# First mixture of experts: a 128-column arm for slots of 128 rows or fewer, and w1 split by column halves

## The chip, the cores and the metric

The kernel runs on one core of a Trainium2 chip. Its engines are TensorE (PE; its weight loads are listed as PEld), VectorE (DVE), ScalarE (ACT), GpSimd (POOL) and SyncE (SP, which only issues transfers). Each has an instruction queue of its own; semaphores order them. The metric is the device time of one execution in microseconds (us).

## The reference

Three layers follow each other, all in float32: a linear attention over 4 x 8 heads of 576 x 64, and two mixtures of experts over N = 2304 rows of 512. The change touches the first mixture, in which some rows are skipped and each of the others goes to one expert:

```python
do_compute = (x @ w_skip) > 0
xc = x[do_compute]
e_idx = argmax(xc @ w_gate)          # one of 8 experts for each row
gate_w = softmax(xc @ w_gate)[e_idx]
h = relu(xc[mask] @ w1[e])           # w1[e]: 512 x 1024
y[mask] = gate_w * (h @ w2[e])       # w2[e]: 1024 x 512
out[do_compute] = xc + y             # the other rows stay x
```

The second mixture is dense, takes most of the time, and starts from the rows that the first one has written to DRAM.

## The kernel before

`moe1` (line 583) works through slots: up to 256 rows (`SLOT`) of one expert. Attention leaves, in DRAM, the rows of x with their gates (`x2d`) and for each expert a list of row numbers (`idx`). Slots 0 and 1 are filled early, from the rows known by then. The others are planned on the chip by `slots` (line 536): first all full slots, those with more than 128 rows (`nfull` of them), then those with 128 or fewer; `nslots` counts both. These two numbers are registers that branches read. `chain` (line 759) nests the slots from 2 up to 17, each under `tc.If(nslots > s - 2)`; the first that fails leaves the chain, and the second mixture begins.

A product in near float32 accuracy is made of three matmuls on a rounded type (float32r): high by high, high by low, low by high, where high is the rounded operand and low the rest. So each operand is split: ACT writes the high half, DVE the low one. In one slot (`slot_body`, line 677):

1. `fetch(s + 1)` lets SP load the next slot's expert weights w1 into `r1` (four transfers, one for each block `kb` of 128 rows of w1) and POOL gather its rows into `xg`. `put(s - 1, 0)` scatters the previous slot's first 128 rows back.
2. First product (lines 690 to 701). For each of 8 blocks `f` of 128 hidden columns, 12 matmuls accumulate `ph`: the weights held by PE are a 128 x 128 block of w1 (`w1h` or `w1l`), the columns streamed are the 256 transposed rows (`xT`: `xTh`, `xTl`). Every matmul has its own weight block. Then ACT writes `hh` = relu(ph) (line 699), DVE its rest `hl` (line 700), and the pair splits block f of the second weights w2 (lines 651 and 652). `ph` has three buffers.
3. `ahead` (line 724): SP loads the next w2 (`fetch2`), and ACT and DVE split the next w1 from `r1` into `w1h`, `w1l` in eight pieces (`split_w1`: piece i is row block i // 2, column half i % 2; half 0 holds blocks f = 0 to 3, half 1 the others). From slot 3 on, `turned(s + 1)` follows: PE transposes the next slot's rows (8 transposes, line 668), ACT and DVE write `xTh` (line 670) and `xTl` (line 671).
4. `product(s, 0)` (line 729): 24 matmuls of 512 columns for the first 128 rows (line 737), and DVE adds gate times result to the rows (line 741).
5. Under `tc.If(nfull > s - 2)` (line 720): `product(s, 1)` and `put(s, 1)` for the second 128 rows.

The slots are under `manual_schedule`: the order of the code is the order on each engine's queue (slot 0 alone is ordered by the scheduler). Where a branch skips a block, the engines bring the semaphore counts of the skipped block up before they go on.

The other lines named below: line 205 is a small plain-float32 matmul in the attention part (128 x 128 weights, 18 columns; `gate_kv`, 2 matmuls in each of 16 calls), line 951 the gate logits of the second mixture (plain float32, 384 columns, 8 weight columns), line 943 its first transposes, lines 1120 and 1359 its main products.

Of the kernel before, what the change touches and what calls it, by code (L numbers as in the profile page):

```python
# [7 lines left out]
F32 = mybir.dt.float32  # L8
# [4 lines left out]
AF = mybir.ActivationFunctionType  # L13
ALU = mybir.AluOpType
# [4 lines left out]
P = 128  # L19
B, H, S, DH, FH = 4, 8, 576, 64, 128  # L20
# [7 lines left out]
SLOT = 256  # L28
# [6 lines left out]
def f32(ap):  # L35
    return ap.bitcast(F32)
# [546 lines left out]
def moe1(tc, nc, c, rt, w1, w2, idx, x2d, second, route, ahead2):  # L583

    with ExitStack() as ctx:
        early = ctx.enter_context(tc.tile_pool(name="m1e", bufs=1, side="right", reuse_waits="tile"))
        NKB, NFB = D // P, FF // P
# [3 lines left out]
        r2 = early.tile([P, NFB, D], F32, name="r2")  # L591
        w1h, w1l = [early.tile([P, NKB, FF], F32R, name=nm) for nm in ("w1h", "w1l")]
# [38 lines left out]
        def fetch(s):  # L631
            e = fetch_w(s)
            fetch_x(s)
            load_r1(e)
            return e
# [7 lines left out]
        def fetch2(e):  # L643
            for f in range(0, NFB, 2):
                nc.sync.dma_start(
                    r2[:, f : f + 2],
                    w2[bass.ds(e, 1), f * P : f * P + 2 * P].rearrange("o (b p) d -> p (o b) d", p=P),
                )

        def split_w(dh, dl, src):  # L650
            nc.scalar.activation(dh, src, AF.Copy)
            nc.vector.tensor_tensor(dl, src, f32(dh), ALU.subtract)

        def split_w1(i, high=True, low=True):
            kb, h = divmod(i, 2)
            sl = slice(512 * h, 512 * h + 512)
            if high:
                nc.scalar.activation(w1h[:, kb, sl], r1[:, kb, sl], AF.Copy)
            if low:
                nc.vector.tensor_tensor(w1l[:, kb, sl], r1[:, kb, sl], f32(w1h[:, kb, sl]), ALU.subtract)  # L660

        def turned(s, ps0=None):
            xg, xT = xgs[s % 3], xTs[s % 2]
            for a in range(2):
                pt = (ps0.tile([P, NKB, P], F32, name="pt", tag="W", bufs=4) if ps0
                      else ps.tile([P, NKB, P], F32, name="pt", tag="T"))
                for kb in range(NKB):
                    nc.tensor.transpose(pt[:, kb], xg[:, a, kb * P : kb * P + P], c["ident"])
                oh, ol = [t[:, :, a * P : a * P + P] for t in xT]
                nc.scalar.activation(oh, pt, AF.Copy)  # L670
                nc.vector.tensor_tensor(ol, pt, f32(oh), ALU.subtract)

        def slot(s):
            with tc.manual_schedule():
                slot_body(s)

        def slot_body(s):
            xT = xTs[s % 2]
            last = s == NSLOT + 1
            if s:  # L680
                put(s - 1, 0)
            if s == 1:
                ahead2()
            if s == 0:
                e = e1
            elif not last:
                e = fetch(s + 1)
            hh = pool.tile([P, NFB, SLOT], F32R, name="hh", tag="hh", bufs=1)
            hl = pool.tile([P, NFB, SLOT], F32R, name="hl", tag="hl", bufs=1)
            for f in range(NFB):  # L690
                ph = ps.tile([P, SLOT], F32, name="ph", tag="H", bufs=3)
                n = 0
                for wt, xt in ((w1h, xT[0]), (w1h, xT[1]), (w1l, xT[0])):
                    for kb in range(NKB):
                        nc.tensor.matmul(
                            ph, wt[:, kb, f * P : f * P + P], xt[:, kb], start=(n == 0), stop=(n == 11)
                        )
                        n += 1
                nc.scalar.activation(hh[:, f], ph, AF.Relu)
                nc.vector.scalar_tensor_tensor(hl[:, f], ph, 0.0, f32(hh[:, f]), ALU.max, ALU.subtract)  # L700
                split_w(w2h[:, f], w2l[:, f], r2[:, f])
            if s < 2:
                ahead(s, e)
            elif not last:
                with tc.If(nslots > s - 1):
                    ahead(s, e)
                    if s > 2:
                        turned(s + 1)
            product(s, 0, hh, hl)
            if s < 2:  # L710
                if s == 0:
                    turned(1)
                for _ in range(3 if s == 0 else 4):
                    ahead2()
                product(s, 1, hh, hl, (lambda: turned(2)) if s else None)
                put(s, 1)
            else:
                if s == 2:
                    turned(3)
                with tc.If(nfull > s - 2):  # L720
                    product(s, 1, hh, hl)
                    put(s, 1)

        def ahead(s, e):
            fetch2(e)
            for i in range(8):
                split_w1(i)

        def product(s, a, hh, hl, between=None):
            xg = xgs[s % 3]  # L730
            py = ps.tile([P, D], F32, name="py", tag="Y")
            n = 0
            for f in range(NFB):
                if between and f == NFB // 2:
                    between()
                for ht, wt in ((hh, w2h), (hl, w2h), (hh, w2l)):
                    nc.tensor.matmul(
                        py, ht[:, f, a * P : a * P + P], wt[:, f], start=(n == 0), stop=(n == 23)
                    )
                    n += 1  # L740
            nc.vector.scalar_tensor_tensor(
                xg[:, a, 0:D], py, xg[:, a, D : D + 1], xg[:, a, 0:D], ALU.mult, ALU.add
            )

        def put(s, a):
            ix, xg = ixs[s % 3], xgs[s % 3]
            ins = nc.gpsimd.indirect_dma_start(
                out=x2d[:, :],
                out_offset=bass.IndirectOffsetOnAxis(ap=ix[:, a].bitcast(U32), axis=0),
                in_=xg[:, a],  # L750
                in_offset=None,
                bounds_check=NTOK - 1,
                oob_is_err=False,
            )
            for o in rt.gathers + rt.written:
                tc.declare_no_dep(ins.ins, o.ins, reason="distinct rows")
            rt.written.append(ins)
# [37 lines left out]
        ps = ctx.enter_context(tc.tile_pool(name="psB", bufs=2, space=PSUM, reuse_waits="tile"))  # L795
        pw = ctx.enter_context(tc.tile_pool(name="psW", bufs=1, space=PSUM, reuse_waits="tile"))
        warm = pw.tile([P, P], F32, name="warm")
        w2h, w2l = [pool.tile([P, NFB, D], F32R, name=nm, bufs=1) for nm in ("w2h", "w2l")]
# [3 lines left out]
        rt.scatter()  # L802
        tabs.extend(rt.slots())
        slot_body(0)
        slot(1)
        ahead2()
        tn = tabs[0]
        nfull = nc.values_load(tn[0:1, 0:1], min_val=0, max_val=NSLOT)
        nslots = nc.values_load(tn[0:1, 1:2], min_val=0, max_val=NSLOT)
# [876 lines left out]
```

## Time and profile before

| | us |
|---|---|
| median of 3 runs | 1932.02 (1930.78 to 1932.33) |
| the profiled execution | 1931.85 |
| its span, first to last instruction | 1930.1 |
| PE busy in the span | 1887.2 |
| DVE, ACT, POOL busy | 1343.9, 930.8, 745.9 |

The profile is that one execution; sums are made against its own time. Attention ends at about 197 us, the slots of the first mixture run from there to 402 us, the second mixture from 409 us to the end. Matmuls are pipelined: the duration of one is its latency, and how fast they go is read from the distance between their starts.

### The profile page before, as it was taken

The numbers are of one execution on the slowest core, as the hardware profiler recorded it, in microseconds if no ns is written. First come the engines' busy times: TensorE is split into PE (matmuls) and PEld (weight loads), VectorE is DVE, ScalarE is ACT, GpSimd is POOL, SyncE is SP. The second block draws the span as 40 slices with busy tenths as digits, with TensorE's granted clock in tenths as the row PEclk, the third lists the DMA queues.
The fourth block names the chain that finished last, engine by engine and source line by source line (L and its number), as shares of the span: only waits on it lengthen the run. The fifth ranks groups of instructions, "written<-read, shape, count | busy, mean of one in ns | idle before, by whom it ended". The sixth has DMA issues, their size and how long they took to land.

```text
span 1930.1 us, 34988 instructions
## 1 busy us (share of the span) xinstructions
PE 1887.2 (98%) x13028; PEld 1778.1 (92%) x13028; DVE 1343.9 (70%) x2309; ACT 930.8 (48%) x1679; POOL 745.9 (39%) x653
## 2 busy tenths in 40 slices
PE   9999999989999999999999999999999999999997
PEld 8998899956889988999899999999999999999997
DVE  5778977664967676767657766767786676676665
ACT  5778655545444444445344444444445444444442
POOL 2012522222433334333124455445563454444445
PEclk9999999999999999999999999999999999999999
DMA  7424686648766767777476676777656766767663
GB/s 196 119 66 164 221 281 220 211 136 288 250 219 243 254 246 245 256 267 269 140 256 224 229 237 217 237 241 251 228 174 232 237 218 232 234 223 246 227 201 110
DMA packets 234691, 422.00 MB, mean 219 GB/s; under 512 B 31594, under 2 KB 151374, under 8 KB 234508
## 3 DMA queue, kind: packets, MB, share of 16 engines
q1 hardware_dynamic: 230892, 412.16, 64.2%
q0 software_dynamic: 3456, 7.40, 1.1%
q8 instruction: 106, 1.74, 0.4%
q14 instruction: 77, 0.63, 0.1%
q10 hardware_dynamic: 160, 0.07, 0.0%
HBM read 311.18 MB, written 110.86 MB: 219 GB/s over the span
## 4 chain that ended last, share of the span: by engine, by line
PE 69%; DVE 3%; POOL 1%; DMA 1%; issue 0%; ACT 0%; POOLq 0%; DVEq 0%; ACTq 0%
PE pu L1359 23%; PE pb L1120 15%; PE py L1155 12%; PE pd L1120 10%; PE pa L1120 9%; POOL acc L1449 1%; POOL hr L1449 0%; DVE hh L1406 0%; DMA w<-wd 0%; DVE wc L884 0%; DVE xcl L1018 0%; DVE acc L1374 0%; DVE hr L1398 0%; DVE hh L1141 0%; DVE acc L1449 0%
## 5 line engine op out<-in xcount | busy, mean ns | idle before, releaser
L1359 PE MATMUL pu<-hh,w 128*128 128x384 f32 x2688 | 541.1, 336 | 8.4 <-DVE acc L1449 4.2
L1359 PEld LDWEIGHTS pu<-hh,w 128*128 128x128 f32 x2688 | 473.9, 188 | 9.4 <-DVE acc L1449 4.6
L1449 POOL TENSOR_TENSOR hr<-hr 128x384 f32<-128x384 f32 (+1 forms) x192 | 282.3, 1470 | 290.0 <-DVE hr L1398 167.6
L1120 PE MATMUL pb<-xch,wc 128*128 128x384 f32 x1152 | 297.7, 339 | 1.8 <-ACT v L1128 0.8
L1402 ACT ACTIVATE hh<-hr 128x384 fp32r<-128x384 f32 (+2 forms) x256 | 189.2, 761 | 204.6 <-POOL hr L1449 152.1
L1155 PE MATMUL py<-w,hh 128*128 128x512 f32 x1152 | 287.5, 396 | 0.0
L1406 DVE TENSOR_TENSOR hh<-hr,hh 128x384 fp32r<-128x384 f32 (+2 forms) x256 | 223.3, 881 | 63.9 <-ACT hh L1402 62.6
L1155 PEld LDWEIGHTS py<-w,hh 128*128 128x128 f32 x1152 | 215.4, 189 | 43.2 <-issue 1.9
L1372 POOL TENSOR_TENSOR acc<-acc,s 128x384 f32<-128x384 f32 x147 | 162.3, 1105 | 224.0 <-ACT s L1371 223.9
L1374 DVE TENSOR_TENSOR acc<-pu,acc 128x384 f32<-128x384 f32 x267 | 147.3, 553 | 103.9 <-PE pu L1359 103.0
L1120 PEld LDWEIGHTS pb<-xch,wc 128*128 128x128 f32 x1152 | 210.2, 188 | 9.7 <-ACT v L1128 1.7
L1120 PE MATMUL pa<-xch,wc 128*128 128x384 f32 x768 | 198.8, 338 | 0.1
L1120 PE MATMUL pd<-xch,wc 128*128 128x384 f32 x768 | 198.0, 338 | 0.5 <-DVE c L1213 0.5
L1371 ACT ACTIVATE s<-pu 128x384 f32<-128x384 f32 x147 | 72.1, 491 | 162.2 <-PE pu L1359 162.0
L1120 PE MATMUL pb<-xcl,wc 128*128 128x384 f32 x576 | 148.8, 339 | 0.0
L1120 PEld LDWEIGHTS pa<-xch,wc 128*128 128x128 f32 x768 | 139.8, 187 | 4.1 <-ACT acc L1102 0.6
L1120 PEld LDWEIGHTS pd<-xch,wc 128*128 128x128 f32 x768 | 140.0, 188 | 1.3 <-DVE c L1213 0.8
L884 DVE TENSOR_TENSOR wc<-r,wc 128x512 fp32r<-128x512 f32 x170 | 130.6, 769 | 3.8 <-ACT wc L881 3.4
L881 ACT ACTIVATE wc<-r 128x512 fp32r<-128x512 f32 x170 | 105.8, 623 | 10.6 <-PE pa L1120 9.2
L1120 PEld LDWEIGHTS pb<-xcl,wc 128*128 128x128 f32 x576 | 104.9, 188 | 0.0
L1120 PE MATMUL pa<-xcl,wc 128*128 128x384 f32 x384 | 99.1, 338 | 0.1
L1120 PE MATMUL pd<-xcl,wc 128*128 128x384 f32 x384 | 99.1, 339 | 0.0
(271 smaller groups left out, 2975.0 us busy)
## 6 DMA issues: line engine op xcount, KB each, us to landing
w<-wd SPq DMA_DIRECT2D x224, 512.0 KB, 4.2
wc<-wd SPq DMA_DIRECT2D x120, 512.0 KB, 4.9
r<-in_moe_w_dram SPq DMA_DIRECT2D x108, 512.0 KB, 4.9
wd<-wc SPq DMA_DIRECT2D x64, 512.0 KB, 3.7
wd<-acc SPq DMA_DIRECT2D x128, 256.0 KB, 3.0
wd<-w SPq DMA_DIRECT2D x96, 256.0 KB, 3.8
r<-in_moe_w_dram SPq DMA_DIRECT2D x90, 256.0 KB, 3.8
acc<-in_moe_w_dram SPq DMA_DIRECT2D x64, 256.0 KB, 3.6
```

The costliest lines, as they stand in the source:

```text
L881: nc.scalar.activation(wc[i][:, 0], wsrc[i], AF.Copy)
L884: nc.vector.tensor_tensor(wc[i][:, 1], wsrc[i], f32(wc[i][:, 0]), ALU.subtract)
L1120: nc.tensor.matmul(dst, wc[i][:, w, kb, sl], xcb[i][x][:, kb], start=(start and m == 0), stop=(stop and m == 5), skip_group_check=True,)
L1155: nc.tensor.matmul(py, ht[:, i * P : i * P + P], w[:, wt], start=(m == 0), stop=(m == 11))
L1359: nc.tensor.matmul(pu, w[:, wl, kb, g2 * P : g2 * P + P], H[:, hx[kb][xl].start + o], start=(m == 0), stop=(m == 5))
L1371: nc.scalar.activation(tmp, pu, AF.Copy)
L1372: nc.gpsimd.tensor_tensor(t, t, tmp, ALU.add)
L1374: nc.vector.tensor_tensor(t, pu, t, ALU.add)
L1402: nc.scalar.activation(H[:, hx[g][0]], R[:, u:v], AF.Copy)
L1406: nc.vector.tensor_tensor(H[:, hx[g][1]], R[:, u:v], f32(H[:, hx[g][0]]), ALU.subtract)
L1449: eng.tensor_tensor(out_, a, b, op)
```

## The change

Slots 2 and up get two arms under one branch on `nfull`: the first for slots of more than 128 rows, the second for the others. Both call a function `rest`, with a width of 256 or 128. The first product (`inner`) streams `width` columns; `hh` and `hl` are written for as many. `ahead` and `product(s, 0)` stand in both arms; `product(s, 1)` and `put(s, 1)` in the wide arm only. Slots 0 and 1 keep 256 columns and their order. `ahead` splits the four pieces of column half 0 first, then calls `between` if there is one (the transposes of the next slot, from slot 3 on), then splits the four pieces of half 1.

```diff
-            for f in range(NFB):
-                ph = ps.tile([P, SLOT], F32, name="ph", tag="H", bufs=3)
...
             if s < 2:
+                inner(xT, hh, hl, SLOT)
                 ahead(s, e)
...
+            def rest(width):
+                inner(xT, hh, hl, width)
+                if not last:
+                    with tc.If(nslots > s - 1):
+                        ahead(s, e, (lambda: turned(s + 1)) if s > 2 else None)
+                product(s, 0, hh, hl)
                 if s == 2:
                     turned(3)
-                with tc.If(nfull > s - 2):
+                if width == SLOT:
                     product(s, 1, hh, hl)
                     put(s, 1)
 
-        def ahead(s, e):
+            with tc.If(nfull > s - 2) as full:
+                rest(SLOT)
+            with full.Else():
+                rest(P)
+
+        def inner(xT, hh, hl, width):
+            sl = slice(0, width)
+            for f in range(NFB):
+                ph = ps.tile([P, SLOT], F32, name="ph", tag="H", bufs=3)[:, sl]
+                n = 0
+                for wt, xt in ((w1h, xT[0]), (w1h, xT[1]), (w1l, xT[0])):
+                    for kb in range(NKB):
+                        nc.tensor.matmul(
+                            ph, wt[:, kb, f * P : f * P + P], xt[:, kb, sl], start=(n == 0), stop=(n == 11)
+                        )
+                        n += 1
+                nc.scalar.activation(hh[:, f, sl], ph, AF.Relu)
+                nc.vector.scalar_tensor_tensor(hl[:, f, sl], ph, 0.0, f32(hh[:, f, sl]), ALU.max, ALU.subtract)
+                split_w(w2h[:, f], w2l[:, f], r2[:, f])
+
+        def ahead(s, e, between=None):
             fetch2(e)
-            for i in range(8):
+            for i in range(0, 8, 2):
+                split_w1(i)
+            if between:
+                between()
+            for i in range(1, 8, 2):
                 split_w1(i)
```

## Rows read from the trace of the kernel before

**Rows 1.** The page: busy us, share and instructions of each engine; chain by engine.
```profile
PE 1887.2 (98%) x13028; PEld 1778.1 (92%) x13028; DVE 1343.9 (70%) x2309; ACT 930.8 (48%) x1679; POOL 745.9 (39%) x653
...
PE 69%; DVE 3%; POOL 1%; DMA 1%; issue 0%; ACT 0%; POOLq 0%; DVEq 0%; ACTq 0%
```

**Rows 2.** Instruction groups, whole span: shapes xcount | busy us, mean ns | idle before, releasers.
```profile
L1359 PE MATMUL pu<-hh,w 128*128 128x384 f32 x2688 | 541.1, 336 | 8.4 <-DVE acc L1449 4.2 <-DVE acc L1374 2.5 <-DMA w<-wd 1.6
...
L699 ACT ACTIVATE hh<-ph 128x256 fp32r<-128x256 f32 x72 | 27.6, 383 | 82.2 <-PE ph L695 50.1 <-issue 32.0
...
L741 DVE SCALAR_TENSOR_TENSOR xg<-py,xg 128x512 f32<-128x512 f32 x16 | 12.0, 748 | 23.5 <-PE py L737 19.2 <-PEq L720 4.3
```

**Rows 3.** Instruction groups from 365 to 402 us (slots 7 and 8).
```profile
L695 PE MATMUL ph<-xTh,w1h 128*128 128x256 f32 x64 | 10.4, 284 | 0.3 <-PEq L720 0.3
...
L700 DVE SCALAR_TENSOR_TENSOR hl<-ph,hh 128x256 fp32r<-128x256 f32 x16 | 6.8, 425 | 5.4 <-ACT hh L699 5.4
```

**Rows 4.** Timeline of PE and its loads: start us, us to the last one's end, xcount.
```profile
273.40 0.55 PEld L695 LDWEIGHTS ph<-xTh,w1h 128*128 128x128 f32 x4
...
273.52 0.64 PE L695 MATMUL ph<-xTh,w1h 128*128 128x256 f32 x4
...
999.78 1.20 PE L1359 MATMUL pu<-hh,w 128*128 128x384 f32 x6
```

**Rows 5.** Waits of PE's loads, 300 to 420 us: total us, times, longest.
```profile
PEld ph L695 <- ACT xTh L670: 0.7, 1, 0.7
...
PEld py L737 <- issue: 0.3, 1, 0.3
```

**Rows 6.** Line 205: timeline around 33 us, and its groups over the whole span.
```profile
33.34 0.52 PEld L205 LDWEIGHTS pgk<-wgd,kvt 128*128 128x128 f32 x4 [0.17 <-ACT kvt L199]
...
33.34 0.62 PE L205 MATMUL pgk<-wgd,kvt 128*128 128x18 f32 x4
...
L205 PE MATMUL pgk<-wgd,kvt 128*128 128x18 f32 x64 | 9.8, 267 | 1.1 <-issue 0.8 <-ACT kvt L199 0.3
...
L205 PEld LDWEIGHTS pgk<-wgd,kvt 128*128 128x128 f32 x64 | 8.3, 190 | 3.8 <-ACT kvt L199 2.7 <-issue 1.1
```

**Rows 7.** Timeline of PE at the start of slot 8; idle before in brackets.
```profile
382.78 0.39 PE L737 MATMUL py<-w2h,hl 128*128 128x512 f32 x1
383.01 0.39 PE L737 MATMUL py<-w2l,hh 128*128 128x512 f32 x1
383.71 0.73 PE L695 MATMUL ph<-xTh,w1h 128*128 128x256 f32 x4 [0.31 <-PEq L720]
384.78 0.74 PE L695 MATMUL ph<-xTl,w1h 128*128 128x256 f32 x4 [0.34 <-DVE xTl L671]
385.35 0.64 PE L695 MATMUL ph<-xTh,w1l 128*128 128x256 f32 x4
```

**Rows 8.** Timeline of ACT and DVE ahead of slot 8.
```profile
377.88 4.27 ACT L658 ACTIVATE w1h<-r 128x512 fp32r<-128x512 f32 x8
382.04 1.07 ACT L670 ACTIVATE xTh<-pt 128x512 fp32r<-128x512 f32 x2
...
378.62 4.90 DVE L660 TENSOR_TENSOR w1l<-r,w1h 128x512 fp32r<-128x512 f32 x8
383.44 1.28 DVE L671 TENSOR_TENSOR xTl<-pt,xTh 128x512 fp32r<-128x512 f32 x2
```

**Rows 9.** Timeline of PE at the start of slot 2.
```profile
248.66 0.73 PE L695 MATMUL ph<-xTh,w1h 128*128 128x256 f32 x4 [0.80 <-issue]
```

**Rows 10.** The page's DMA queues: packets, MB, share; a DMA group: KB, us to landing.
```profile
q8 instruction: 106, 1.74, 0.4%
...
wg<-in_moe_w_gate_dram SPq DMA_DIRECT2D x1, 16.0 KB, 1.9
```

**Rows 11.** Line 951 over the whole span, an instruction group.
```profile
L951 PE MATMUL pg<-xq,wg 128*8 128x384 f32 x16 | 5.5, 486 | 0.0
```

**Rows 12.** Windows: us, busy of PE, PEld, DVE, ACT, POOL, granted clock, DMA share, GB/s.
```profile
401.50:409.40 7.90, 0.41 (x3) 0.04 (x1) 0.75 (x1) 0.00 (x0) 1.03 (x1) 0.80 0.22 51
```

More of the change, by code (lines that the diff above doesn't have):

```diff
@@ L689, in slot_body @@
             hl = pool.tile([P, NFB, SLOT], F32R, name="hl", tag="hl", bufs=1)
-            for f in range(NFB):
-                ph = ps.tile([P, SLOT], F32, name="ph", tag="H", bufs=3)
[L692 to L701, printed above, removed]
             if s < 2:
+                inner(xT, hh, hl, SLOT)
                 ahead(s, e)
[L704 to L710, printed above, removed]
+                product(s, 0, hh, hl)
                 if s == 0:
@@ L716, in slot_body @@
                 put(s, 1)
-            else:
+                return
+            def rest(width):
[3 more added lines that the diff above has]
+                        ahead(s, e, (lambda: turned(s + 1)) if s > 2 else None)
+                product(s, 0, hh, hl)
                 if s == 2:
                     turned(3)
-                with tc.If(nfull > s - 2):
+                if width == SLOT:
                     product(s, 1, hh, hl)
                     put(s, 1)
-        def ahead(s, e):
-            fetch2(e)
-            for i in range(8):
+            with tc.If(nfull > s - 2) as full:
[17 more added lines that the diff above has]
+        def ahead(s, e, between=None):
+            fetch2(e)
+            for i in range(0, 8, 2):
[3 more added lines that the diff above has]
+            for i in range(1, 8, 2):
                 split_w1(i)
```

## The prediction, made before the changed kernel was run

> **What bounds the kernel now.** I read the page's busy table and its chain first [rows 1]: TensorE (PE) is busy for 98% of the span and carries 69% of the chain that ended last, no other engine more than 3%. So a stage gets shorter only where PE gets shorter or stops waiting, and whatever a stage saves reaches the end, because the stages behind it are bound by PE too. The page covers 1930.1 us; the profiled execution took 1931.85 us, 1.75 more around the span, and the median of the three runs is 1932.02. I sum against 1931.85; it stands 0.17 below the median.
>
> Next the instruction groups of the stage that the diff touches [rows 2, 3]. The Relu of line 699 occurs 72 times, 8 to a slot, so nine slots ran; line 741 closes a `product` and occurs 16 times, 2 × 7 + 2, so seven slots made two products and two made one. A single product means 128 rows or fewer. The change therefore meets two slots; the timeline puts them last, slots 7 and 8, from 365.1 to 401.9 us. In that stretch line 695 has 64 matmuls of each of its three kinds, 192 in all, 96 a slot, each streaming 256 columns of which at most 128 hold rows.
>
> Then the timeline of PE, for the interval between matmuls, since a single duration (284 ns) is latency and overlaps the next. Four matmuls of 256 columns take 0.64 us to the end of the last: (0.64 − 0.284)/3 = 119 ns; their weight loads, of 0.19 each, start (0.55 − 0.19)/3 = 120 ns apart [rows 3, 4]. With 384 columns six take 1.20 us, the last one 0.336: 173 ns [rows 2, 4]. With 512 columns two starts are 0.23 us apart [rows 7]. From 384 to 256 columns that is 0.42 ns a column, with 13 ns besides, and 512 lies on the same line.
>
> Last the waits of PE from 300 to 420 us [rows 5] and the timeline where they fall [rows 7]: at the start of slot 8 PE waits for its own queue behind a skipped branch (0.31), for xTh from ScalarE (ACT) and for xTl from VectorE (DVE); ahead of slot 8's product, where another branch is skipped, its loads idle 0.3. Slot 7 begins, and the wide slots follow each other, without a listed wait.
>
> **The change part by part.**
>
> *128 columns instead of 256.* The straight line would give 0.42 × 128 + 13 = 67 ns. But each of these matmuls has weights of its own, 128 x 128, and the loads have to keep up. The trace has no matmul of this rounded type under 256 columns. The nearest rows are the plain f32 matmuls of line 205: weights of the same shape, a load of the same 190 ns, and only 18 columns to stream. Their loads still start (0.52 − 0.19)/3 = 110 ns apart, the matmuls (0.62 − 0.267)/3 = 118 ns [rows 6]. The load alone sets that pace. So I expect 110 ns, not 67: 192 × (120 − 110) = 1.9 us less. The bounds by these rows are 1.9 and 0 (at 118 to 120 ns); a gain outside them, 67 ns, and a loss, several passes per column, are rivals below. I take 110 since at 256 columns the stream itself needs 120, which may hide a faster load, and 110 is the only pace seen where the stream is out of the way. The narrower Relu and line 700 (0.38 and 0.42 us now) get shorter, which changes nothing: per f block DVE needs 0.42 and a split of 4.90/8, 1.0 us [rows 3, 8], ACT 0.38 and 4.27/8, 0.9 [rows 2, 8], PE 12 × 0.110 = 1.32, so PE still sets the pace.
>
> *The split of w1 by column halves, with the transposes between.* At the start of slot 8, PE's last product matmul starts at 383.01, the next is due at 383.24. It comes at 383.71 (+0.47); the second group of four is due 0.48 later and comes at 384.78 (+0.59); the third is due at 385.26 and comes at 385.35 (+0.09): 1.15 us lost [rows 7]. The reason is the order on ACT and DVE: eight splits, then xTh from 382.04 for 1.07, then xTl from 383.44 for 1.28 [rows 8]. With four splits first, ACT is through at 377.88 + 4.27/2 = 380.0 and xTh at 381.1; DVE is through at 378.62 + 4.90/2 = 381.1 and xTl at 382.4; both precede 383.24. The four odd splits end at about 383.2 on ACT and 384.8 on DVE and are first read at f = 4, 48 matmuls or 5.3 us into the slot. So these two waits go. What is late next is PE's own queue: the skipped second product at the end of slot 7 costs 0.31 as now [rows 7] (it lay within the wait for ACT), and the new skip of the wide arm another 0.31, by the skip ahead of slot 8's product [rows 5]. 1.15 − 0.62 = 0.5 us less. SyncE (SP)'s loads of r1 rows are queued behind the later splits, because row kb now comes free only after the odd half: about 2 to 4 us later, landing in about 4 us, more than 10 us ahead of their use in the next `ahead`. In the wide slots a second product (24 × 0.23 = 5.5 us) covers the order either way: nothing. Slots 0 and 1 have no transposes between; their order is changed at no cost, the same eight pairs under a product.
>
> *The arms.* Ahead of slot 7, PE's queue must jump over slot 6's narrow arm and then over slot 7's wide arm: two skips at 0.31, +0.6. Ends of slots 2 to 5 jump over a narrow arm each; now they pass the end of a block with no wait listed, and PE has a product of 5.5 us at hand there: 0. At the first dynamic slot PE already idles 0.80 with nothing shown that it waits for [rows 9]; one more branch there, +0.1, an eighth of it, as an estimate.
>
> What speaks against this is code size. The queue of instruction packets moved 106 packets with 1.74 MB [rows 10], 16.4 KB each; PE has 13028 matmuls and as many loads, many times any other engine's [rows 1], so this is its queue, with about 67 bytes to each of the 26056 and some 245 to a packet. The wide arm is 96 + 8 + 48 = 152 matmuls, 304 instructions, more than a packet; the narrow one 128, or 256. No row shows a jump of that length with PE's fetch visible by itself. Bounds: 0, as the passed block ends show; and per jump one packet, for which the nearest row is the 16 KB load of wg, 1.9 us to landing [rows 10], or two, 3.8. I keep 0.31 per skip, the row of an actual skip, and keep 3.8 for a rival. [...]
>
> *Sum.* −1.9 − 0.5 + 0.6 + 0.1 = −1.7: 1931.85 − 1.7 = 1930.15, predicted 1930.2.
>
> **The rivals.**
>
> *The stream sets the pace.* If the load of the rounded type is faster than that of line 205, the interval falls to 67 ns: 192 × 53 = 10.2 us. DVE and ACT (8 × 1.0 = 8 us a slot at most, and less at half width) trail PE's 6.4, but the product of 5.5 us follows and hides that. With the other terms (+0.2) 1921.9. For: the straight line from 512 to 256. Against: line 205, and loads of the rounded type with the same 190 ns. [...]
>
> *Short streams lose the single pass: slower.* A plain f32 matmul of 384 columns keeps PE busy 5.5/16 = 344 ns [rows 11], 0.9 ns a column, and each product takes two such instructions (line 205's 16 × 2 matmuls stand as 64 [rows 6]). If a rounded matmul under 256 columns falls to both, 128 columns cost 2 × 0.9 × 128 = 230 ns: 192 × 110 = 21.1 us more, 1953. It decides from 120 ns an interval, measurably from about 141. For: no shorter stream of this type stands in the trace. Against: nothing in the instruction changes but the count.
>
> *Jumps wait for code: slower.* Each of the two jumps over a wide arm waits for two packets: 2 × 3.8 − 1.9 − 0.5 + 0.1 = +5.3, 1937.2. For: the arm's 304 instructions. Against: slot 7's jump has slot 6's second product (5.5 us) in flight.
>
> *The change does nothing* because no slot has 128 rows or fewer: excluded by the 16 products of rows 2.
>
> **How the numbers follow.** Forecast 65%, the stream 9%, several passes 12%, jumps 9%; 5% for what I do not see, among it a stretch of half clock behind the chain that begins elsewhere (between 401.5 and 409.4 us PE idles and the mean grant is 0.80 [rows 12]). The forecast's own range is 1928.3 to 1933. Range 1926.5 to 1937: it leaves out the fully streamed case and the several passes, and holds what lies between forecast and jumps. About 0.2% (3.9 us) is what a measurement can tell from no change. Faster by more: 9% plus some of the forecast's edge and the clock, 0.15. Slower by more: 12% plus most of the jumps, 0.20. Within: 0.65.
>
> **What would show it.** In the changed profile, line 695's 192 narrow matmuls at a mean interval near 110 ns, their loads back to back; no wait of slot 8 for xTh or xTl; 0.6 us of queue idle on PE ahead of slots 7 and 8. An interval near 67 or 230 ns would show a rival and make the prediction wrong, as would PE idle of 2 us or more ahead of slot 7 or 8 with no engine named, or a wait of a wide slot for line 741.

## The result: slower by 0.5%, and the profile after

The changed kernel takes 1941.82 us (median; 1940.34 to 1943.56), the kernel before 1932.05 in the same comparison (1928.77 to 1934.76): ratio 1.0053, interval 1.0040 to 1.0066. The forecast was 1930.2, its range ended at 1937. The profiled execution took 1941.6, its span is 1939.9.

In the page PE is busy longer at the same number of instructions [rows 1], and seven more packets of instructions were fetched [rows 10]:

```profile
PE 1895.8 (98%) x13028; PEld 1786.4 (92%) x13028; DVE 1344.9 (69%) x2309; ACT 928.1 (48%) x1679; POOL 747.0 (39%) x653
...
q8 instruction: 113, 1.85, 0.4%
...
PE 68%; DVE 3%; POOL 1%; DMA 1%; ACT 1%; issue 1%; POOLq 0%; DVEq 0%; ACTq 0%; SPq 0%
```

Lines have moved: the first product is line 726 (695 before), the product over w2 751 (737), its DVE step 755 (741), the width branch 714, the second mixture's transposes 957 (943). PE's waits from 240 to 425 us (total, times, longest):

```profile
PE pt L957 <- DMA acc<-x2d: 6.6, 1, 6.6
PE ph L726 <- issue: 4.8, 2, 3.6
PE ph L726 <- DVE xg L755: 0.4, 1, 0.4
```

The waits for xTh and xTl [rows 5, 7] are gone. In their place stands 3.6 us of "issue": PE idle, and nothing shown that it waits for. The timeline of PE says where (start, us to the last one's end, idle before in brackets); it answers to rows 4, 7 and 9:

```profile
250.06 0.73 PE L726 MATMUL ph<-xTh,w1h 128*128 128x256 f32 x4 [1.23 <-issue]
...
273.48 0.64 PE L726 MATMUL ph<-xTh,w1h 128*128 128x256 f32 x4
274.49 0.74 PE L726 MATMUL ph<-xTl,w1h 128*128 128x256 f32 x4 [0.36 <-DVE xg L755]
...
367.04 0.39 PE L751 MATMUL py<-w2l,hh 128*128 128x512 f32 x1
370.99 0.96 PE L726 MATMUL ph<-xTh,w1h 128*128 128x128 f32 x4 [3.56 <-issue]
371.75 1.05 PE L726 MATMUL ph<-xTl,w1h 128*128 128x128 f32 x4
372.60 1.05 PE L726 MATMUL ph<-xTh,w1l 128*128 128x128 f32 x4
...
399.27 0.40 PE L751 MATMUL py<-w2l,hh 128*128 128x512 f32 x1
399.50 0.56 PE L726 MATMUL ph<-xTh,w1h 128*128 128x128 f32 x4
399.90 0.61 PE L726 MATMUL ph<-xTl,w1h 128*128 128x128 f32 x4
400.34 0.61 PE L726 MATMUL ph<-xTh,w1l 128*128 128x128 f32 x4
```

The idle is ahead of slot 7. Behind it four narrow matmuls take 0.85 us from start to start, 213 ns each; in slot 8 they take 0.447, 112 ns each, near the forecast 110. The windows give the reason (us, busy of PE, PEld, DVE, ACT, POOL, granted clock, DMA share, GB/s):

```profile
248.00:371.00 123.00, 117.85 (x769) 107.47 (x767) 82.12 (x140) 61.90 (x130) 32.16 (x31) 1.00 0.69 243
371.00:395.00 24.00, 24.00 (x109) 23.61 (x110) 9.74 (x20) 8.95 (x22) 2.88 (x3) 0.50 0.26 87
395.00:416.00 21.00, 20.85 (x141) 18.79 (x139) 12.77 (x24) 8.91 (x21) 4.06 (x4) 1.00 0.41 132
```

PE is busy for all of 371 to 395 us, but at a granted clock of 0.50. Before, the clock was full from 248 to 402 us.

Where the time went, from the starts of each stage in both timelines (us):

| stage | before | after | stage longer by |
|---|---|---|---|
| slot 2 starts | 248.66 | 250.06 | +1.4 |
| slot 7 starts | 365.35 | 370.99 | +4.2 |
| slot 8 starts | 383.71 | 399.50 | +10.2 |
| slot 8's last product matmul | 401.51 | 415.77 | -1.5 |
| second mixture's transposes | 409.39 | 422.79 | -0.9 |
| end of the span | 1930.1 | 1939.9 | -3.6 |

Of the first +1.4, 0.43 is idle ahead of slot 2; the other 1.0 came earlier, in a stretch (190 to 248 us) with a granted clock of 0.97, where before has 1.00; some profiles of the experiments have it and some have not. The last -3.6 lies in the second mixture, which was not changed: its length differs by as much between profiled executions (1520.7 before, 1517.1 after, 1515.4 in `e7` below). I have not followed these two further. Of the rest, slots 7 and 8 are the subject.

### The profile page after: what moved, and what is told of

It is laid out like the page before. It is cut to its first block, busy times and chain, and to the rows that moved or that the text cites. A ratio compares the mean times of both kernels' runs of the same rounds, so it can differ in the third digit from the quotient of the medians.

```text
span 1939.9 us, 34964 instructions
## 1 busy us (share of the span) xinstructions
PE 1895.8 (98%) x13028; PEld 1786.4 (92%) x13028; DVE 1344.9 (69%) x2309; ACT 928.1 (48%) x1679; POOL 747.0 (39%) x653
## 4 chain that ended last, share of the span: by engine, by line
PE 68%; DVE 3%; POOL 1%; DMA 1%; ACT 1%; issue 1%; POOLq 0%; DVEq 0%; ACTq 0%; SPq 0%
PE pu L1373 22%; PE pb L1134 14%; PE py L1169 12%; PE pd L1134 9%; PE pa L1134 9%; POOL acc L1463 0%; POOL hr L1463 0%; DVE hh L1420 0%; DMA acc<-in_moe_w_dram 0%; DVE hh L1155 0%; DVE wc L898 0%; DVE xcl L1032 0%; DMA w<-wd 0%; DVE acc L1388 0%; DVE hr L1412 0%
```

## The experiments

**Theory, jump and clock.** To get from slot 6's wide arm to slot 7's narrow arm, PE's queue jumps over slot 6's narrow arm and at once over slot 7's wide arm, and waits for instructions. PE runs dry for 3.6 us, the clock falls to 0.50, and in 20 us matmuls of 128 columns don't get it back. **Rivals:** narrow streams lower the clock by themselves; the new order of the split costs; any taken jump does it; code loading, not idle, lowers the clock.

| run | median us | before, same chip | ratio, 95% interval |
|---|---|---|---|
| e1 columns only | 1928.74 | 1931.83 | 0.9987 (0.9979 to 0.9996) |
| e2 arms, 256 columns | 1934.31 | 1931.83 | 1.0016 (1.0008 to 1.0025) |
| e3 order only | 1930.89 | 1931.83 | 0.9996 (0.9987 to 1.0005) |
| e4 short arms | 1932.45 | 1931.83 | 1.0011 (0.9996 to 1.0026) |
| e5 columns and order | 1932.00 | 1932.97 | 0.9993 (0.9982 to 1.0004) |
| e9 idle, no jump | 1947.07 | 1932.97 | 1.0066 (1.0051 to 1.0081) |
| e8 narrow arm first | 1933.77 | 1932.97 | 1.0016 (1.0001 to 1.0031) |
| e6 busy through the jump | 1933.32 | 1932.97 | 1.0004 (0.9994 to 1.0014) |
| e7 second product out | 1936.30 | 1929.59 | 1.0026 (1.0013 to 1.0040) |
| e10 slot 8 at 256, with a second product | 1947.35 | 1929.59 | 1.0093 (1.0078 to 1.0108) |
| e11 two fillers ahead of slot 8 | 1928.05 | 1929.59 | 0.9989 (0.9979 to 1.0000) |
| e12 one filler | 1927.42 | 1931.14 | 0.9981 (0.9972 to 0.9990) |
| e13 slot 8 at 256 | 1931.83 | 1931.14 | 1.0010 (1.0001 to 1.0020) |

### One part at a time

**e1, columns only**, on the kernel before:

```diff
+            sl = slice(0, SLOT if s < 7 else P)
...
-                            ph, wt[:, kb, f * P : f * P + P], xt[:, kb], start=(n == 0), stop=(n == 11)
+                            ph, wt[:, kb, f * P : f * P + P], xt[:, kb, sl], start=(n == 0), stop=(n == 11)
```

> The kernel before, with the first product's columns fixed in the code: 256 for slots 0 to 6 and 128 for slots 7 and 8 (right for these inputs, which have two slots of 128 rows or fewer). No arms, the old order of the split. Theory 'jump and clock' (PE's jump over slot 7's wide arm stalls its queue, and the idle of 3.6 us lets the clock fall to half for slot 7): nothing here jumps farther than before, so the granted clock stays 1.0 from 248 to 402 us, the narrow matmuls come every 110 ns in both slots, and the time is 1932.05 - 192 x 0.010 = 1930.1. Rival 'narrow streams' (128 columns by themselves keep PE too little busy, and the clock falls without any idle ahead): half clock in slot 7, in slot 8 or in both, matmuls every 213 ns there, 96 x 0.103 = 10 us more for each, 1940 or more.

As the theory said. Slot 7's first product runs at full clock, and four matmuls take 0.447 us from start to start (365.34, 365.79, 366.24), 112 ns each. The window holds nearly all of that product:

```profile
364.78:375.17 10.39, 10.39 (x96) 10.39 (x95) 7.18 (x15) 5.58 (x14) 5.82 (x5) 1.00 0.57 170
```

So here narrow streams with no idle ahead kept the clock, at 1.00. The gain is 2.5 us by the ratio (0.8 to 4.1), but it is not that of the columns alone: the waits for xTh and xTl are absent here too, with the old order, since the narrower Relu and hl alone (0.28 and 0.29 us in the changed kernel, 0.38 and 0.43 before) bring ACT and DVE through in time. From slot 7's start to slot 8's last product matmul the profile shows 34.13 us instead of 36.16; of these 2.0 the 192 shorter intervals are 1.5.

**e3, order only**, on the kernel before:

```diff
-            for i in range(8):
+            for i in range(0, 8, 2):
+                split_w1(i)
+            if between:
+                between()
+            for i in range(1, 8, 2):
                 split_w1(i)
```

> The kernel before with only the new order of the next slot's w1: even column halves, then the transposes, then the odd halves. No arms, 256 columns everywhere. Jump and clock: the waits of slot 8 for xTh and xTl go (1.15 us lost before, 0.31 left for the skip that lay under them), no idle over 1 us ahead of slot 7, clock 1.0 from 248 to 402 us: 1931.2. Rival 'order' (the later odd halves or the later r1 loads hold up a slot): a new wait of line 695's loads for w1 ahead of or within slots 3 to 8, and a time above 1932.

Inconclusive in time: 0.9 less by the medians, an interval on both sides of 1. In PE's waits from 240 to 425 us the two of slot 8 are gone and no new one for w1 has come, so the rival falls:

```profile
PE ph L695 <- issue: 0.6, 1, 0.6
PE ph L695 <- PEq L718: 0.3, 1, 0.3
```

**e2, arms with 256 columns**, on the changed kernel:

```diff
-                inner(xT, hh, hl, width)
+                inner(xT, hh, hl, SLOT)
```

> The changed kernel with 256 columns in the second arm too: the arms, their jumps and the new order stay, only the narrow streams go. Jump and clock: PE idles 3.6 us ahead of slot 7 as in the changed kernel and the clock falls to half there; with 240 ns a matmul (twice 120) through the whole first product that is 3.6 + 96 x 0.12 = 15 us, less the 0.5 to 1.1 us of slot 8's waits, 1946; if the wider streams get the clock back halfway, 1940. Narrow streams: the idle stays but the clock doesn't fall, 1932.05 + 3.6 - 1 + 0.3 = 1935.

The idle stays (3.58 us) and the clock falls, without any narrow stream; but it comes back after 6 us in the midst of the first product, not after 24. The windows: idle, the half clock (four matmuls in 0.853 us, 213 ns each, in the timeline), the rest (four in 0.476, 119 each):

```profile
367.10:370.67 3.57, 0.00 (x0) 0.03 (x1) 0.75 (x1) 0.00 (x0) 2.20 (x3) 0.90 0.75 288
370.67:376.79 6.12, 6.12 (x29) 6.12 (x30) 1.32 (x3) 1.52 (x4) 2.88 (x3) 0.50 0.17 57
376.79:384.88 8.09, 8.09 (x70) 8.09 (x69) 6.10 (x12) 4.80 (x11) 0.00 (x0) 1.00 0.40 130
```

Both expectations of the theory were too high: the median is 2.5 over before, and the profiled execution (1939.67) is the slowest of the twelve. By the median alone the rival's 1935 would have been met; it is the profile that shows the fall, and whether the other eleven had it, their granted clocks (0.990 to 0.995 over the whole execution) don't tell. What tells the parts apart is the sum: arms and jump with wide columns +2.5 by the medians, narrow columns alone -3.1, together +9.8. The two don't add; they meet in the clock.

**e5, columns and order**: `e1` with the order of `e3`.

> Columns fixed in the code as in the columns-only run (128 for slots 7 and 8, right for these inputs) plus the new order of the split; no arms. What the change would be without its jumps. Jump and clock: no idle over 1 us ahead of slots 7 and 8, clock 1.0 until the chain, 1931.8 - 3.1 (columns alone, measured) - 0.9 (order alone, measured) = 1927.8 if the two add; 1928.7 if the narrower Relu and hl had already freed ACT and DVE ahead of slot 8, so that the order has nothing left to hide. Rival 'narrow streams by themselves': some executions near 1940, as 3 of the 12 of the short arms had, with half clock in slot 8.

The two gains don't add: 1.0 less than before, the interval at both sides of 1, and between 1927.3 and 1935.1 no upper group; in the profile the clock is full through slots 7 and 8, as the theory said. Since `e1` had lost slot 8's waits without the order, there was nothing left for it. Whether the order costs something beside narrow columns these runs don't tell.

### Idle or jump

**e9, idle without a jump**: `e5` with this behind slot 6's second product:

```diff
+                    if s == 6:
+                        xh = xTs[1][0]
+                        for w in (NKB, NKB, 1):
+                            nc.vector.tensor_tensor(xh[:, 0:w], f32(xh[:, 0:w]), f32(xh[:, 0:w]), ALU.max)
```

> The kernel with fixed columns and the new order, and one pause: behind slot 6's last product VectorE writes slot 7's xTh onto itself (two passes of 1024 columns and one of 256, some 2.6 us behind its 0.75 us for xg), so that PE idles about 3.5 us ahead of slot 7, as in the changed kernel, with no jump of code. Jump and clock says that the idle makes the clock fall and the 128-column streams keep it down, whatever caused the idle: half clock for some 24 us from slot 7's start, matmuls every 213 ns, and 1928 + 3.5 + 10 = 1941.5. Rival 'the jump itself' (code loading, not idle, lowers the clock): clock 1.0, matmuls at 110 ns, 1928 + 3.5 = 1931.5.

The clearest run. PE waits 3.79 us, for DVE this time, and the narrow matmuls behind it go at half clock, 97 in 20.09 us (timeline of PE, then the windows):

```profile
372.49 0.66 PE L696 MATMUL ph<-xTh,w1h 128*128 128x128 f32 x4 [3.79 <-DVE xTh L725]
...
368.70:372.49 3.79, 0.00 (x1) 0.03 (x1) 3.53 (x4) 0.00 (x0) 2.41 (x2) 1.00 0.48 192
372.49:392.58 20.09, 20.09 (x97) 20.09 (x97) 6.89 (x14) 5.57 (x14) 3.41 (x4) 0.51 0.28 96
```

Against `e5`'s timeline slot 7 starts 3.9 us later (372.49 to 368.63) and slot 8 15.0 later (401.42 to 386.46): 11.1 us for the clock, where I had put 10. The median rises by 15.1. Idle of another cause does it too; no jump over an arm is needed.

**e6, busy through the jump**: the changed kernel with ten fillers at the end of slot 6's wide arm (`warm` widened to 512 columns):

```diff
+                    if s == 6:
+                        for _ in range(10):
+                            nc.tensor.matmul(warm, c["ident"], f32(w2h[:, 0]), start=True, stop=True)
```

> The changed kernel with ten plain f32 matmuls of 512 columns into an unused PSUM tile at the end of slot 6's wide arm (work that the result doesn't need), so that PE has work in hand while its queue jumps. Each is two instructions of about 0.46 us, 9.2 us in all. Jump and clock: PE idles 1 us or less ahead of slot 7, the clock stays 1.0, slot 7's matmuls come every 110 ns: 1932 - 2.5 + 9.2 = 1938.7, less than the changed kernel for 9 us more work. Rival 'narrow streams' (they lower the clock whatever is ahead): half clock in slot 7 all the same, 1941.8 - 3.6 + 9.2 = 1947.

The fillers take 8.2 us, and the clock stays. The windows of the fillers and of slot 7's first product:

```profile
367.17:375.35 8.18, 8.18 (x21) 3.63 (x20) 0.75 (x1) 0.00 (x0) 5.08 (x5) 1.00 0.51 186
375.35:386.42 11.07, 11.07 (x98) 10.83 (x97) 6.51 (x14) 5.58 (x14) 0.00 (x0) 1.00 0.28 95
```

With 8 us of useless work added, the kernel takes 1933.32 instead of 1941.82. From the end of slot 6's products to slot 8's start it is 25.6 us (367.17 to 392.81) instead of 32.2 (367.27 to 399.50): idle and clock had cost more than the work that hides them. The branch into slot 7's arm still takes 4.95 us here, all of it under the fillers. The expected 1938.7 was too high by 5 us, of which the shorter fillers (8.2, not 9.2) are one. The rest stays open, and the edit did a second thing: the 16 transposes into `warm` that run ahead of slot 2 elsewhere (246.0 to 247.6 before) now ran behind the chain (409.9 to 411.6), probably because the fillers write the same tile. Slot 2 started 23.4 us after slot 1 instead of the changed kernel's 26.5; by slot 6 0.4 us of that was left. What the move is worth behind the chain no run shows by itself.

### Where the arms stand

**e8, narrow arm first**, on the changed kernel:

```diff
-            with tc.If(nfull > s - 2) as full:
-                rest(SLOT)
-            with full.Else():
+            with tc.If(nfull < s - 1) as small:
                 rest(P)
+            with small.Else():
+                rest(SLOT)
```

> The changed kernel with its two arms swapped in the code: the narrow one stands first, the wide one in the Else. From slot 6's wide arm PE now runs straight into slot 7's narrow arm; before, it jumped over slot 6's narrow arm and at once over slot 7's wide arm. Slot 7 to slot 8 still jumps over a wide arm, a single jump, which took 0.42 us of the queue in the changed kernel. If it is the two jumps in a row that stall PE: no idle over 1 us ahead of slots 7 and 8, clock 1.0 through slot 7, 1929 to 1930 with general widths, with perhaps a few executions near 1940 as with the short arms. Rival (any jump over the longer wide arm stalls): 3.6 us of idle ahead of slot 8 in place of slot 7, half clock there, 1941.

No idle ahead of slot 7, 0.68 us ahead of slot 8, full clock in both (timeline of PE at the two starts):

```profile
366.91 0.56 PE L726 MATMUL ph<-xTh,w1h 128*128 128x128 f32 x4
...
384.80 0.63 PE L726 MATMUL ph<-xTh,w1h 128*128 128x128 f32 x4 [0.68 <-issue]
```

From 359 to 376 us the queue of instruction packets moved one packet in `e8` (packets, MB, share):

```profile
q8 instruction: 1, 0.02, 0.4%
```

and three in the changed kernel:

```profile
q8 instruction: 3, 0.05, 2.0%
```

The trace's records of PE's branch instructions, which the views leave out, show what is hidden and what is not. The changed kernel's branch into slot 7's narrow arm starts at 363.68 and takes 7.14 us, while PE's last product matmul starts at 367.04: about half is covered. Two of the three packets move inside that branch; they start at 366.75 and 366.79, 3.1 us into it, and land at 368.59 and 368.87, 2.0 us before it ends (the queue from 363.68 to 370.82 us):

```profile
q8 instruction: 2, 0.03, 3.4%
```

In `e8` the branch ahead of slot 8, where one wide arm is passed, still takes 4.47 us, but starts at 379.88, under the product; one packet moves inside it. The pattern holds in all fifteen traces: between 240 and 425 us 28 branches of PE took more than 1 us, and during each one or two packets were moving; of the 491 shorter ones 30 saw one. So the long branches go with packets on the queue of instructions. A jump over one arm can be slow too (4.47 us here); the two in a row took longer (7.14) than the work that PE had at hand (3.4). The median is 8 us below the changed kernel's but not below before: 8 of 12 executions took 1929.7 to 1935.2, four 1938.1 to 1942.5. The granted clock of the whole execution, on record for each, is 0.987 to 0.989 in three of these four, as in all six of the changed kernel (0.986 to 0.989), and 0.991 to 0.994 in the other nine. So three executions look like falls of the clock, and the fourth (1939.2 at 0.993) does not.

**e7, second product out**: the changed kernel with `product(s, 1)` and `put(s, 1)` under an `If` of their own behind both arms.

> The changed kernel with the second product taken out of the wide arm into a branch of its own behind both arms, as before. The order of the arms stays: wide first, narrow in the Else. Slot 6 now ends with that product (5.5 us), and the two jumps are no longer back to back: the one over slot 6's narrow arm comes ahead of the product, only the one over slot 7's wide arm (some 262 PE instructions) behind it. If two jumps in a row make the stall: idle under 1 us ahead of slot 7, clock 1.0 through slot 7's first product, median about 1931, a few executions near 1940. Rival (any jump over the wide arm stalls, and the swapped arms escaped because none stood ahead of slot 7): 3.6 us of idle ahead of slot 7 and 1941 in nearly all executions.

Neither expectation held. Slot 7 starts on time, but 16 matmuls into it PE idles 1.22 us with nothing shown that it waits for, and behind that the clock falls (timeline of PE):

```profile
366.63 0.61 PE L726 MATMUL ph<-xTh,w1h 128*128 128x128 f32 x4
368.46 0.96 PE L726 MATMUL ph<-xTl,w1h 128*128 128x128 f32 x4 [1.22 <-issue]
369.22 1.05 PE L726 MATMUL ph<-xTh,w1l 128*128 128x128 f32 x4
```

The windows up to the end of that pause, and from there to the end of the first product, at a grant of 0.51:

```profile
365.34:368.46 3.12, 1.90 (x17) 1.76 (x15) 1.73 (x3) 0.80 (x2) 1.58 (x2) 1.00 0.76 303
368.46:385.40 16.94, 16.94 (x80) 16.94 (x81) 5.91 (x12) 4.77 (x12) 3.88 (x4) 0.51 0.33 116
```

Ten of twelve executions took 1934.5 to 1939.4, two 1926.7 and 1928.2. Only one of them has a profile, but the granted clocks of the whole executions, 0.988 to 0.991 in the ten and 0.994 in the two, agree with the one group having the fall and the other not. Ahead of slot 8 PE idles 0.80 us in this profile, and there the clock stays full.

**e4, short arms**: the changed kernel with arms around `inner` alone; `ahead` and the products behind them for both.

> The changed kernel with arms around the first product alone (96 matmuls in either); the split of the next w1 and the first product over w2 stand behind them for both, the second product in a branch of its own as before. A jump over the wide arm now passes some 195 PE instructions instead of some 311. Jump and clock, where the distance passed makes the stall: idle under 1 us ahead of slots 7 and 8, clock 1.0 through slot 7, matmuls every 110 ns, 1932.05 - 1.9 - 0.5 = 1929.6, or up to 1931 if each block adds 0.3. Rival 'any arm' (a taken jump into a second arm stalls whatever its length): 3.6 us of idle ahead of slot 7 and half clock behind it again, 1941.

No idle ahead of slot 7 and full clock in it, 1.00: this jump into an arm did not stall. Three of the twelve executions took 1939.6 to 1944.7 and nine 1928.9 to 1933.2; the profiled one is of the three. Their granted clocks are 0.986 to 0.989, those of the nine 0.991 to 0.995. In the profiled one the clock falls in slot 8, less than 3 us behind an idle of 0.79:

```profile
383.17 0.66 PE L723 MATMUL ph<-xTh,w1h 128*128 128x128 f32 x4 [0.79 <-PEq L712]
...
385.01 0.61 PE L723 MATMUL ph<-xTl,w1h 128*128 128x128 f32 x4
385.46 0.79 PE L723 MATMUL ph<-xTh,w1l 128*128 128x128 f32 x4
386.05 1.05 PE L723 MATMUL ph<-xTh,w1h 128*128 128x128 f32 x4
```

The windows of the first products of slots 7 and 8, at 1.00 and 0.57:

```profile
365.17:375.84 10.67, 10.67 (x97) 10.67 (x96) 7.25 (x15) 5.57 (x14) 5.82 (x5) 1.00 0.61 214
383.17:401.40 18.23, 18.23 (x96) 18.23 (x96) 8.15 (x16) 5.57 (x14) 4.05 (x4) 0.57 0.37 125
```

### Slot 8, and a version that beats both

**e10** was meant to give slot 8 256 columns in `e8`, by `rest(P if s == 7 else SLOT)`.

> The kernel with the narrow arm first, but 128 columns for slot 7 alone; slot 8's narrow arm streams 256 (widths by slot number in the code). The swapped arms had four executions of twelve between 1938.1 and 1942.5. If these are the clock falling in slot 8, where PE idles 0.7 us just ahead of narrow streams: they go or shrink to about half (256 columns get the clock back within 7 us), all executions below 1938, and the fast ones lose half of the columns' gain, 96 x 0.010 = 1 us. Rival (the clock falls in slot 7, or behind the chain, whatever slot 8 does): as many executions above 1938 as with the swapped arms, 1 in 3.

It didn't answer: `rest(SLOT)` brings the second product along, so slot 8 made two, and the narrow arm of every other slot grew by one, which the wide slots jump over. That shows in PE's waits from 240 to 425 us, five in place of two:

```profile
PE ph L726 <- issue: 6.8, 5, 2.4
```

Its branches over these longer arms take 4.37 and 6.41 us, and two of the pauses make a pair: 2.35 us in slot 2 (until 254.25) leave the clock full, 2.37 ahead of slot 5 (until 324.44) are followed by half clock for 3.4 us, with 256 columns behind either.

**e13, slot 8 at 256 columns** does it with one product: `inner(xT, hh, hl, SLOT if s == 8 else width)` in `e8`.

> The kernel with the narrow arm first; slot 8's first product streams 256 columns, nothing else changed (one product in slot 8, as it should; the run with both products in it did not answer this). PE idles 0.7 us ahead of slot 8 as with the swapped arms. Jump and clock: no upper group or one within 3 us, since streams of 256 columns get the clock back within 7 us; the others 1 us above the swapped arms with 128 columns, ratio to before 0.9995. Rival (the upper group comes from slot 7 or from behind the chain): 1 execution in 3 more than 5 us above the median, as with the swapped arms.

PE idles 0.98 us ahead of slot 8, and the twelve executions lie between 1928.4 and 1937.6 without a group apart; one is more than 5 us above the median, but none has a granted clock below 0.992. The median is 0.7 above before, that of `e8` was 0.8 above.

**e11 and e12, fillers ahead of slot 8**: `e8` with two, then one, of `e6`'s fillers behind slot 7's product.

> The kernel with the narrow arm first and two plain f32 matmuls of 512 columns into an unused PSUM tile behind slot 7's product (1.7 us of work that the result doesn't need), to cover the 0.7 us of idle ahead of slot 8. Jump and clock: no idle over 0.4 us ahead of slot 8, no execution above 1938, the others up by 1.7 - 0.7 = 1 us: median 1932 to 1933. Rival (narrow streams lower the clock by chance without any idle): as many executions near 1940 as with the swapped arms, 1 in 3.

> The kernel with the narrow arm first and one plain f32 matmul of 512 columns (two instructions, some 0.8 us of work that the result doesn't need) behind slot 7's product instead of two. Jump and clock: the filler still covers most of the 0.7 us of idle ahead of slot 8, no execution in the upper group (more than 5 us above the median), and the time is 0.4 to 0.8 us below that with two fillers: ratio to before 0.9985. Rival (fillers matter by the time they shift, not by the idle they cover): an upper group of about 1 in 3 comes back.

In `e12` PE goes from the product through the filler into slot 8 with no idle listed, and the clock stays full:

```profile
383.64 0.40 PE L754 MATMUL py<-w2l,hh 128*128 128x512 f32 x1
383.87 1.02 PE L715 MATMUL warm<-w2h,ident 128*128 128x512 f32 x2
384.33 0.96 PE L729 MATMUL ph<-xTh,w1h 128*128 128x128 f32 x4
```

The window of slots 7 and 8:

```profile
365.00:402.00 37.00, 36.24 (x259) 33.07 (x257) 23.67 (x45) 17.87 (x42) 10.37 (x9) 1.00 0.50 174
```

None of the 22 executions of the two lies above 1933.2 or has a granted clock below 0.992, against three executions that look like falls among the 12 of `e8`. So what looks like falls in `e8` needs the idle ahead of slot 8 (gone in `e11`, `e12`) and, less surely, its narrow streams (gone in `e13`, where none of 12 against three of 12 can be chance). That they lie in slot 8 is taken over from `e4`'s profile; none of the three was profiled.

The filler of `e12` did not remove that idle by covering it. The same jump over slot 7's wide arm that takes 4.47 us in `e8` and 4.76 in `e13` takes 0.29 in both `e11` and `e12`, and in `e12` it ends at 380.5, 3 us before PE starts the filler; no packet moves inside it. Why it is short there is not shown. And these two have the moved transposes of `e6` as well: slot 2 starts 23.4 us after slot 1 instead of `e8`'s 26.5, of which 0.9 us (`e12`) and 0.3 (`e11`) are left at slot 7's start.

`e12`, with widths chosen on the chip as in the changed kernel, is the version that beats both: 0.9981 of before (0.9972 to 0.9990), 3.7 us (1.9 to 5.4). Its profile has 2.0 of it in slots 7 and 8 (34.19 us from slot 7's start to slot 8's last product matmul, for 36.16 before; `e8` has 34.26); how much of the rest the moved transposes bring is open. Its filler stands at slot 7 by number in the code, which is right for these inputs only.

## Why the prediction was wrong

**128 columns, -1.9: right, a little high.** 112 ns at full clock for 120 before, 1.5 us for 192; the 2.5 of `e1` (0.8 to 4.1) holds slot 8's two waits as well. The pace is near the 110 ns of line 205's loads [rows 6]; that the load sets it no run tests.

**The split by halves, -0.5: right in what it removes, not shown in time.** The waits for xTh and xTl are gone, and ahead of slot 8 no idle is listed where I had left 0.62: the branch there took 0.42 us under PE's product. But narrower columns alone remove them too (`e1`).

**The arms, +0.6: the step that failed.** I priced the two skips ahead of slot 7 at 0.31 each, from skips that pass eight transposes [rows 5] and 24 matmuls [rows 7], where the wide arm has 152, and set the rival that jumps wait for code at 9% with the argument that "slot 7's jump has slot 6's second product 5.5 us in flight". The branch came late in that product: 3.4 us before its last matmul started, and it took 7.14. 3.56 us of idle came out instead of 0.6, for slot 7 alone, since slot 8's jump was hidden; it is the idle of 2 us or more that I had named as a sign of being wrong. That it is near the rival's 3.8 for a jump is luck: that price was two packets of 1.9 us in a row, while the two packets moved side by side in 2.1 us, the branch took another 5 around them, and the product covered half.

**What no rival had: the clock.** The prediction looked for half clock only behind the chain [rows 12], as something "that begins elsewhere". The idle of the jump rival and the narrow streams of the forecast, each priced alone, cost together what neither does. Slot 7 starts 3.7 us late (370.99, due 367.27), and from its start to slot 8's start it takes 28.5 us where `e8`, without its 0.68 of idle, takes 17.2: 11.3 for the clock. With +1.4 and +0.5 ahead of that and -1.2 and -1.5 for what the change was to save in slots 7 and 8, slot 8's last product matmul comes 14.3 us later, as the table has it.

**Slots 2 to 5, 0, and slot 2, +0.1: a little low.** Slot 2 idles 1.23 us instead of 0.80 [rows 9], and slot 3 waits 0.36 us for line 755 (741 before), one of the signs I had named.

## What to carry to other kernels

Price a jump over a long arm by what the engine still has in its queue when the branch is reached (3.4 us of the product for a branch of 7.14 in the changed kernel), not by the length of the stage before it (5.5), and put the arm that follows on without a jump where that queue is short (in `e8` no idle stood ahead of slot 7, in the changed kernel 3.56). Before streams are shortened, look at what idle stands ahead of them: in `e9` a pause of 3.8 us cost 15 where 128-column streams followed. Where such a pause can't be removed, work that nobody needs may be the cheaper choice: in `e6` 8.2 us of it made the stretch that it stands in 6.6 us shorter. And look whether such work moves other work, as it moved the transposes into `warm`.

## What the runs showed of the hardware

- Idle of 3.6 (jump) and 3.8 us (DVE), and of 1.2 (`e7`) and 0.8 (`e4`), was followed by a granted clock of 0.50 to 0.51 (0.57 over `e4`'s window, the first 2.5 us of which are at full clock); by the granted clocks of whole executions in ten of twelve in `e7` and in three of twelve in `e4`. The length of the idle doesn't settle it: 1.23 us ahead of slot 2, with 256 columns behind it, left the clock full in the changed kernel, as did 0.80 ahead of slot 8 in `e7` with 128 columns.
- Once at half clock, 128-column matmuls with a weight block each stayed there although PE was busy throughout: 20.4 us of them in the changed kernel, where the clock came back at 395.0, 2.1 us into the matmuls of 512 columns that followed. With streams of 256 columns it was back after 6.1 us (`e2`).
- At half clock matmuls of 128 and of 256 columns come at the same 213 ns; at full clock at 112 and 119 to 120.
- A taken branch of PE took 0.42 us (the changed kernel, ahead of slot 8), 4.47 (`e8`) and 7.14 (the changed kernel, ahead of slot 7), with no packet of instructions moving inside it, one, and two. What makes one short and another long I can't tell from these runs: in the changed kernel the jump over slot 8's wide arm took 0.42, in `e8` a jump over a wide arm 4.47, and in `e12` the same jump 0.29.
